# Two orders in a fused attention and gated-FFN kernel: the last v, q and k products of a chunk with their PSUM banks, and the step of an exchanged gate piece

## The chip, the cores and the metric

The kernel runs on one core of one Trainium2 chip. The metric is the device time of one execution in microseconds (us). Times are lower-is-better, and the time before is the median of three runs.

## The reference

One input `x` of 1 x 2048 x 576 in bf16. It is layer-normed, goes through a sliding-window attention of 32 heads of 18 with a window of 256, and through a gated FFN with 4608 hidden columns; the two results are multiplied.

```python
xn = _layernorm(x)
q, k, v = split(xn @ wqkv)                       # 32 heads of 18
p = softmax(mask(q @ k.T * 18 ** -0.5))          # causal, window 256
s = (p @ v) @ wo
g = silu((sigmoid(xn @ w_gate) * (xn @ w_up)) @ w_down)
return x + s * g
```

## The kernel before

**Chunks.** The 2048 tokens are worked in four chunks (c = 0 to 3) of 512 tokens, each of four blocks of 128. A chunk goes through these stages on TensorE (PE): the q, k and v products (line 521), the first FFN product with gate and up (f1, line 898) with the attention's scores (line 688) and the product of probabilities and v (line 745) put between its steps, then the second FFN product (f2, line 1045) with the output projection `wo` (line 815) inside it. The stages of neighbouring chunks overlap: the q, k, v products of chunk c+1 stand between the two halves of f2 of chunk c, that is, behind f2 of blocks 0 and 1 and ahead of f2 of blocks 2 and 3. So there are three such transitions, from chunk 0 to 1, 1 to 2 and 2 to 3.

**One order for all engines.** `schedule` (line 1145) is a list planner. Every operation has an engine, a cost, a priority (a smaller number goes first, at 40 ns a step) and dependencies; each engine takes next the operation that can start first by these costs, and this order is then fixed in the program (`emit`, line 1288). At run time an engine waits on semaphores in that order and does not skip.

**Banks.** PSUM has eight banks of 512 f32 a partition. A `Psum` object lists candidate banks, and the planner takes the candidate that is free first by its costs (`place`, line 1180); of two that are free at the same time it takes the first listed. A bank is free when its last reader is done.

**The transition.** `build_qkv` (line 543) issues twelve products of 1.1 us each, one after the other (`QKV_CHAIN`), in the order of `QKV_NEXT`; q2 waits in order for the second half of `wo` (`QKV_WO`), so six products (to k1) stand ahead of that half and six behind it. Each product takes two banks: (4,5), (6,7), (0,1) or (2,3), unless `QKV_BANKS` gives it a list of its own. What empties the banks differs:

- q is copied by VectorE (DVE) in one piece of 128x576, k by ScalarE (ACT) in one such piece (line 579). Both go into a ring `pk` of three slots, and SyncE (SP) then issues a DMA that transposes the slot into `qkp` (line 604). A slot is free again when its transposing DMA has landed, so the copy of a q or k waits for the DMA of three products of q and k before.
- v is copied in four pieces of 64x288, two by ACT and two by DVE (line 625), into `vau`; no DMA is involved.
- `kd` (line 672) are DVE operations that need the transposed k of two blocks. Those of the first head group on k0 and k1 stand in DVE's order shortly behind the copies of v2, with priority 0 where a copy has 1.

**f2 of blocks 2 and 3** (`build_f2_pair`, line 1029) takes the banks `F2B = ((0, 1), (2, 3))`, both pairs at its first matmul. It runs 17.6 us, and f1 of the next chunk follows, in banks 4 to 7. After the two transposes of q3 and k3, SP issues the loads of the first three weight groups of that f1, twelve DMAs.

**f1** (`build_ffn`, line 858) works in steps: a step is one matmul on rows 0 to 63 of the array (list `low`, the gate tiles) and one on rows 64 to 127 (list `high`, the up tiles), nine steps for a tile of 128 hidden columns. Since 576 is nine pieces of 64, gate and up do not split evenly, and two pieces of one gate tile, number `XS[c]` (13 in chunk 0, 1 in the others), are exchanged into `high`, with weights from `sat`:

```python
n = NC * (xs - 1) + XP[0]
high[n:n] = [(0, xs, 0, 0), (0, xs, 1, 1)]
```

From that step on the gate tile holds a bank of 4 to 7. The steps are issued in runs of two or three, which begin where a tile changes in either list (`cuts`); a run waits at its start for all its weights, for new banks and for a fence: the gate tile's own first run in `low` waits until the exchanged matmuls in `high` are complete. The four loads of a weight group are for rows 0 to 63 positions 0 to 4, rows 64 to 127 positions 0 to 3, then 5 to 8 and 4 to 8. A bank of f1 is emptied by a tanh on ACT (line 912) for gate, and by a multiplication on DVE (line 916) for up.

The scores are released by steps of f1: in chunks 1 to 3 the first after f2 is over, the second behind the first run that begins at step 7 or later, then every 7 steps. They take the banks (0,1) and (2,3).

Of the kernel before, what the change touches and what calls it, by code (L numbers as in the profile page):

```python
# [59 lines left out]
AVOID_NS = 20000.0  # L60
RBN = 4
XS = (13, 1, 1, 1)
XP = (4, 0)
RUN = 3
WX_PRIO = -1
WX_FT = 7
WD_AT = (14, 18, 22, 28, 29, 30, 31, 32, 33)
QKV_FIRST = "q0 q1 v0 v1 q2 v2 k0 v3 k1 q3 k2 k3"
QKV_NEXT = "q0 k0 q1 v0 v1 k1 q2 k2 v2 q3 k3 v3"
QKV_GATE = 2  # L70
QKV_PRIO = -2
QKV_CHAIN = 1
QKV_WO = {"v1": (0,), "q2": (1,)}
WO_QKV = {"k0": (1,)}
QKV_BANKS = {"q3": ((0, 1), (2, 3)), "k3": ((4, 5), (6, 7)), "v3": ((4, 5), (6, 7))}
QKV_F2 = (1, 8)
LAST = 448
W_GATE = 2
# [138 lines left out]
class Builder:  # L217
# [325 lines left out]
    def build_qkv(self, c):  # L543
        self.op_q, self.op_k, self.op_qkt, self.op_qe = [], [], [], []
        old = [o for l in self.op_sc[c - 1] for o in l] + self.op_tail if c > 0 else []
        order = QKV_FIRST if c == 0 else QKV_NEXT
        prev = None
        for w in order.split():
            i, j = int(w[1]), "qkv".index(w[0])
            o = (self.build_v if j == 2 else self.build_qk)(c, i, j, old)  # L550
            if c > 0:
# [5 lines left out]
                for ps in o.alloc:  # L557
                    ps.cands = QKV_BANKS.get(w, ps.cands)
            prev = o
# [298 lines left out]
    def build_ffn(self, c):  # L858
# [7 lines left out]
        for ft in range(NFT):  # L866
            low += [(0, ft, i, None) for i in (gp if ft == xs else range(NC))]
            high += [(1, ft, i, None) for i in (up if ft == xe else range(NC))]
        n = NC * (xs - 1) + XP[0]
        high[n:n] = [(0, xs, 0, 0), (0, xs, 1, 1)]  # L870
        n = len(low) - NC + XP[1]
        low[n:n] = [(1, xe, 0, 0), (1, xe, 1, 1)]
# [534 lines left out]
```

## Time and profile before

| what | us |
|---|---|
| median of three runs (559.4, 560.35, 560.78) | 560.35 |
| the profiled execution | 559.34 |
| its span, first to last instruction | 557.6 |
| around the span | 1.74 |
| PE busy | 551.9 (99% of the span) |
| DVE busy, ACT busy | 312.2, 279.5 |
| q, k, v products, DVE copy of one q | 0.752 (median) |
| DVE copy of one piece of v, ACT copy of one piece of v | 0.458, 0.407 (medians) |
| one `kd` on DVE | 0.281 (median) |

The profiler records one execution. A row of the timeline has its start, its length, the engine, the line of the kernel, the operation with the tiles it writes and reads, the shapes, and in brackets the idle time of that engine before it with what ended it. PEld is the loading of weights into PE, which runs beside its matmuls; "issue" there means that PE's own queue held it. Two matmuls of a step begin within some ns of each other, and the next step begins about 0.216 later when nothing holds it (45.59 and 45.80 in chunk 0).

### The profile page before, as it was taken

How to read it: one execution, taken by the hardware profiler on the slowest of the kernel's cores; microseconds unless marked ns; L12 is line 12 of the kernel's file. 1: busy time of each engine (PE TensorE's matmuls, PEld its weight loads, DVE VectorE, ACT ScalarE, POOL GpSimd, SP SyncE). 2: the span in 40 equal slices, each digit the busy share in tenths (PEclk: the TensorE clock that was granted, in tenths of full speed). 3: DMA queues.
4: the chain of work that ended last, by engine and by line, in shares of the span. 5: the costliest groups of instructions: out<-in, count | busy, mean ns of one | idle time of the engine just before them, and what ended most of it. 6: DMA issues, size and time to landing. Idle time of an engine off the chain costs nothing.

```text
span 557.6 us, 18763 instructions
## 1 busy us (share of the span) xinstructions
PE 551.9 (99%) x8146; PEld 309.8 (56%) x8146; DVE 312.2 (56%) x906; ACT 279.5 (50%) x395; POOL 29.3 (5%) x58
## 2 busy tenths in 40 slices
PE   8999999999999999999999999999999999999997
PEld 5755555567555455556755554545665555554554
DVE  6436998415067988633407798852330785975011
ACT  8436886124076767602308778740330875883021
POOL 3000110100000100010000011001000000000100
PEclk9999999999999999999999999999999999999999
DMA  8999878938945676234993666423399356660010
GB/s 201 221 203 210 209 183 224 232 62 154 209 104 128 148 152 137 53 52 66 176 206 87 151 149 150 105 51 73 60 178 190 90 127 144 133 132 25 20 44 22
DMA packets 125929, 73.35 MB, mean 132 GB/s; under 512 B 54680, under 2 KB 125336, under 8 KB 125848
## 3 DMA queue, kind: packets, MB, share of 16 engines
q1 hardware_dynamic: 125848, 72.16, 61.1%
q8 instruction: 64, 1.05, 0.8%
q14 instruction: 17, 0.14, 0.1%
HBM read 55.48 MB, written 2.36 MB: 104 GB/s over the span
## 4 chain that ended last, share of the span: by engine, by line
PE 98%; DVE 1%; DMA 0%; issue 0%; ACT 0%
PE ps L898 50%; PE ps L1045 22%; PE ps L521 9%; PE ps L688 6%; PE ps L745 4%; PE ps L815 3%; PE ps L1076 2%; PE ps L1100 2%; DMA xr<-in_A_x_dram 0%; DVE bnst L460 0%; DVE bnst L458 0%; DVE xnr L469 0%; PE ps L495 0%; DVE mv L462 0%; ACT expr L1133 0%
## 5 line engine op out<-in xcount | busy, mean ns | idle before, releaser
L898 PE MATMUL ps<-xn,wgs 64*128 64x512 bf16 x2522 | 299.3, 376 | 0.0
L898 PEld LDWEIGHTS ps<-xn,wgs 64*128 64x128 bf16 x2522 | 121.5, 94 | 114.1 <-issue 1.4
L703 ACT ACTIVATE expr<-ps 128x1024 bf16<-128x1024 f32 (+1 forms) x152 | 150.7, 1019 | 23.9 <-PE ps L688 23.8
L916 DVE SCALAR_TENSOR_TENSOR hT<-tring,ps 128x512 bf16<-128x512 bf16 x144 | 98.2, 682 | 54.8 <-PE ps L898 35.1
L912 ACT ACTIVATE tring<-ps 128x512 bf16<-128x512 f32 x144 | 86.5, 600 | 82.3 <-PE ps L898 62.5
L1045 PE MATMUL ps<-wd_sb,hT 64*128 64x512 bf16 (+1 forms) x2016 | 125.5, 283 | 0.1
L1045 PEld LDWEIGHTS ps<-wd_sb,hT 64*128 64x128 bf16 x2016 | 65.8, 94 | 58.8 <-issue 0.4
L717 DVE TENSOR_TENSOR expr<-expr,m 128x256 bf16<-128x256 bf16 (+1 forms) x272 | 61.3, 267 | 6.4 <-ACT expr L703 5.9
L688 PE MATMUL ps<-qkp,kd 64*128 64x320 bf16 (+4 forms) x720 | 56.7, 252 | 0.0
L521 PE MATMUL ps<-wqkv_sb,xn 64*128 64x288 bf16 x864 | 54.4, 283 | 0.0
L688 PEld LDWEIGHTS ps<-qkp,kd 64*128 64x128 bf16 x720 | 34.2, 94 | 33.3 <-issue 0.8
L672 DVE TENSOR_SCALAR kd<-qkp,hm 128x256 bf16<-128x256 bf16 x176 | 40.5, 290 | 15.7 <-DMA qkp<-pk 13.4
L1133 ACT ACTIVATE expr<-ps 128x576 bf16<-128x576 f32 (+2 forms) x17 | 9.8, 620 | 76.9 <-PE ps L1045 61.6
L521 PEld LDWEIGHTS ps<-wqkv_sb,xn 64*128 64x128 bf16 x864 | 42.8, 94 | 9.4
L1135 DVE SCALAR_TENSOR_TENSOR expr<-expr,ps 128x576 bf16<-128x576 bf16 x12 | 8.5, 751 | 66.6 <-ACT expr L1133 66.6
L840 ACT ACTIVATE sat<-ps 128x576 bf16<-128x576 f32 x16 | 9.5, 648 | 65.1 <-PE ps L815 65.1
L1137 DVE TENSOR_TENSOR expr<-expr,sat 128x576 bf16<-128x576 bf16 (+2 forms) x17 | 7.2, 436 | 43.5 <-ACT expr L1133 34.4
L761 DVE STREAM_TRANSPOSE pk<-ps 128x512 f32<-128x512 f32 x32 | 21.4, 696 | 17.2 <-PE ps L745 17.2
L727 POOL COPY qkp<-qkp 128x256 bf16<-128x256 bf16 x24 | 10.2, 427 | 263.7 <-DVE kd L672 263.7
L778 DVE STREAM_TRANSPOSE op__63<-pk 128x512 bf16<-128x512 bf16 x32 | 22.3, 701 | 0.1
L745 PEld LDWEIGHTS ps<-expr,vau 64*32 64x32 bf16 x1440 | 18.1, 92 | 7.4 <-issue 5.5
L745 PE MATMUL ps<-expr,vau 64*32 64x320 bf16 (+4 forms) x1440 | 20.8, 254 | 0.0
(55 smaller groups left out, 222.7 us busy)
## 6 DMA issues: line engine op xcount, KB each, us to landing
wgs<-in_B_w_gate_dram SPq DMA_DIRECT2D x47, 240.0 KB, 3.8
wgs<-in_B_w_up_dram SPq DMA_DIRECT2D x47, 240.0 KB, 4.8
wgs<-in_B_w_up_dram SPq DMA_DIRECT2D x47, 192.0 KB, 4.3
wgs<-in_B_w_gate_dram SPq DMA_DIRECT2D x47, 192.0 KB, 4.7
wd_sb<-in_B_w_down_dram SPq DMA_DIRECT2D x9, 576.0 KB, 6.4
xf<-in_A_x_dram SPq DMA_DIRECT2D x18, 144.0 KB, 2.6
out_dram<-xf SPq DMA_DIRECT2D x15, 144.0 KB, 2.1
xr<-in_A_x_dram SPq DMA_DIRECT2D x14, 144.0 KB, 4.3
```

The source lines that it names most:

```text
L521: r = e.matmul(self.bank(ps, HV, hf), self.xn[r0:r0 + 64, k, i * P:(i + 1) * P], self.wqkv_sb[r0:r0 + 64, j, k, :], start=(k == 0), stop=( ...
L672: return e.tensor_scalar(dst, src, self.hm[:, half:half + 1], None, ALU.mult)
L688: i = e.matmul(self.bank(ps, 512, r)[:, pos * 64:(pos + n) * 64], w, self.qkp[r0:r0 + 64, hg, q0 * 64:(q0 + n) * 64], start=True, stop=Tru ...
L703: return e.activation(self.expr[:, es, :, 0:ncol], src, ACTF.Exp, scale=SM_SCALE)
L717: return e.tensor_tensor(ap, ap, m, ALU.mult)
L745: r = e.matmul(self.bank(ps2[s_])[32 * cg:32 * cg + 32, q0 * 64:(q0 + n) * 64], vf[:, v0:v0 + 32], self.expr[p0:p0 + 64, es, cg % 2, pos * ...
L761: tr = self.rd("DVE", dve_ns(CH), lambda e, tf=tf, s_=s_: e.transpose(tf, self.bank(ps2[s_])), f"t1:{c}:{t}", deps=[o, self.op_mul[c][t - ...
L778: t2 = self.op("DVE", dve_ns(CH), lambda e, on=on: e.transpose(self.op_[:, hg % NOT, :], on.rearrange("p g d -> p (g d)")), f"t2:{c}:{hg}" ...
L898: return e.matmul(self.bank((pg, pu)[gu][ft]), w, self.xn[r0:r0 + 64, i, :], start=first, stop=last, tile_position=(r0, 0))
L912: return e.activation(self.tring[:, st_, :], self.bank(ps), ACTF.Tanh, scale=0.5)
L916: return e.scalar_tensor_tensor(self.hT[:, ft, :], self.tring[:, st_, :], 1.0, self.bank(ps), ALU.add, ALU.mult)
L1045: r = e.matmul(self.ps[:, b + n0:b + n1], self.hT[r0:r0 + 64, ft, i * P:(i + 1) * P], self.wd_sb[r0:r0 + 64, q, ft % WDG, n0:n1], start=(s ...
```

## The change

Three constants change. In the three later chunks v3 is computed ahead of q3 and k3. The bank lists of the last products are exchanged: v2 and v3 may now use only (0,1) and (2,3), those of f2 of blocks 2 and 3; q3 and k3 only (4,5) and (6,7), those of f1. And the two exchanged pieces of gate stand one step later in `high`, behind five instead of four pieces of the up tile, in all four chunks.

```diff
-XP = (4, 0)
+XP = (5, 0)
-QKV_NEXT = "q0 k0 q1 v0 v1 k1 q2 k2 v2 q3 k3 v3"
+QKV_NEXT = "q0 k0 q1 v0 v1 k1 q2 k2 v2 v3 q3 k3"
-QKV_BANKS = {"q3": ((0, 1), (2, 3)), "k3": ((4, 5), (6, 7)), "v3": ((4, 5), (6, 7))}
+QKV_BANKS = {"v2": ((0, 1), (2, 3)), "v3": ((0, 1), (2, 3)), "q3": ((4, 5), (6, 7)), "k3": ((4, 5), (6, 7))}
```

## The prediction

> **What bounds the kernel.** I read the page's busy times first, then the chain and PE's waits, then the timeline where the change cuts in.
>
> ```profile
> span 557.6 us, 18763 instructions
> PE 551.9 (99%) x8146; PEld 309.8 (56%) x8146; DVE 312.2 (56%) x906; ACT 279.5 (50%) x395; POOL 29.3 (5%) x58
> ...
> PEclk9999999999999999999999999999999999999999
> ...
> PE 98%; DVE 1%; DMA 0%; issue 0%; ACT 0%
> ```
>
> ```profile
> PE ps L396 <- DVE hm L381: 1.5, 1, 1.5
> PE ps L495 <- DVE xnr L469: 0.4, 1, 0.4
> PE ps L495 <- DVE mv L462: 0.3, 1, 0.3
> ```
>
> PE is the bound from end to end, at full clock, and the only waits that the profile lists for it (second fence, from the list of waits) are in the first 8 us. But a matmul's end is modelled, so a short wait hides inside "busy". I therefore compared the starts of neighbouring matmuls with their normal pace (0.216 a step of f1, 0.122 a pair of q, k, v). Outside the first 8 us and the v products of the attention, which lose the same time in every group, only two places lose over 0.1 us. Both lie where the change cuts in. The first is in f1 of chunk 0, at gate tile 13:
>
> ```profile
> 44.84 0.60 ACT L912 ACTIVATE tring<-ps 128x512 bf16<-128x512 f32 x1 [1.34 <-PE ps L898]
> ...
> 45.02 0.09 PEld L898 LDWEIGHTS ps<-xn,wgs 64*128 64x128 bf16 x1
> 45.55 0.09 PEld L898 LDWEIGHTS ps<-xn,wgs 64*128 64x128 bf16 x1 [0.44 <-issue]
> ...
> 45.59 0.39 PE L898 MATMUL ps<-xn,sat 64*128 64x512 bf16 x1
> ```
>
> The `sat` matmul is the exchanged piece. Its run needs the bank that the tanh of gate 11 empties at 45.44. PE's queue is held until then, the weights load at 45.55, and the step starts at 45.58; the step before started at 45.22, so 0.36 - 0.216 = **0.15 us** are lost. The second is f2 of blocks 2 and 3 at the transition from chunk 1 to 2:
>
> ```profile
> 273.74 0.48 DVE L672 TENSOR_SCALAR kd<-qkp,hm 128x256 bf16<-128x256 bf16 x2 [1.00 <-DMA qkp<-pk]
> ...
> 274.25 0.76 DVE L579 CAST pk<-ps 128x576 bf16<-128x576 f32 x1
> ...
> 274.68 0.65 ACT L579 ACTIVATE pk<-ps 128x576 bf16<-128x576 f32 x1 [2.04 <-DMA qkp<-pk]
> ...
> 275.13 0.36 PEld L1045 LDWEIGHTS ps<-wd_sb,hT 64*128 64x128 bf16 x6 [0.38 <-issue]
> 275.16 0.61 PE L1045 MATMUL ps<-wd_sb,hT 64*128 64x512 bf16 x4
> ```
>
> f2 waits for the copy of q3 (DVE, 274.25, over at 275.01), which sits in (2,3). That copy is late: v2 was copied from 271.79, q3's product was ready one product (1.10) later, near 272.9, but two `kd` stand ahead of it and wait until 273.72 for the transposed k1. The last q, k, v pair started at 274.77, so f2 was due at 274.90 and lost **0.26 us**. The other two transitions have the same order and lose nothing:
>
> ```profile
> 135.76 0.48 DVE L672 TENSOR_SCALAR kd<-qkp,hm 128x256 bf16<-128x256 bf16 x2 [0.30 <-DMA qkp<-pk]
> 136.27 0.76 DVE L579 CAST pk<-ps 128x576 bf16<-128x576 f32 x1
> ...
> 137.61 0.59 PE L1045 MATMUL ps<-wd_sb,hT 64*128 64x512 bf16 x4
> ...
> 410.33 0.48 DVE L672 TENSOR_SCALAR kd<-qkp,hm 128x256 bf16<-128x256 bf16 x2
> 410.85 0.76 DVE L579 CAST pk<-ps 128x576 bf16<-128x576 f32 x1
> ...
> 412.46 0.59 PE L1045 MATMUL ps<-wd_sb,hT 64*128 64x512 bf16 x4
> ```
>
> So 0.41 us is all that the two places can give back.
>
> **The change, part by part.**
>
> *Exchanged piece one step later.* The matmuls are the same; one up step goes ahead of two exchanged ones. In chunk 0 the piece is then due one step later, at 45.43 + 0.216 = 45.65, and the bank lets it start at 45.58: the whole 0.15 goes (bounds: 0 and -0.15). Two waits move. The run of three steps now waits for the group's fourth weight load four steps earlier; in chunk 0 those loads land by 37.6, 7 us ahead, and in chunk 1 by 147.8 against an f1 that starts at 155.25. And the fence is nearer: three steps, 0.648, from the last exchanged matmul to the gate tile's own first, instead of four. It needs the matmul's 0.376 and then some 0.135 from a semaphore to a matmul (45.44 to 45.58 above), 0.51 in all, so 0.14 is left: nothing. In chunks 1 to 3 a score unit of 0.22 stands between as well, and the bank at step 4 had been free for long: nothing either way. The score's gate at step 7 opens one run earlier, but its banks are free only when DVE has read blocks 2 and 3 of f2 (two multiplications from 156.14 to 157.56), and the second unit starts at 157.84 already: nothing.
>
> *v3 ahead of q3 and k3.* Product 10 of 12 is now v3. v2's shorter list changes nothing: it takes (0,1), the first to come free behind `wo`. v3 takes what q3 took, (2,3); q3 follows `wo` into (4,5), and k3 gets (6,7), which q2 or k2 has left. f2 now waits for v2 and v3 instead of v2 and q3. v3 is ready at the same time as q3 was, near 272.9, with the same priority, so in DVE's order I expect it **behind the same two `kd`**. Its DVE part is two copies of 0.458 with 0.03 between, 0.95, for one copy of 0.76: +0.19. ACT's two pieces (0.407 each) stand ahead of k3's copy and are done by 273.8. Per transition: 1 to 2 starts f2 at 275.16 + 0.19 = 275.35 and loses 0.45; 0 to 1 has the second copy done at 136.27 + 0.95 = 137.22, and the weights of f2 load from 137.49: 0.27 in hand; 2 to 3 has it at 410.85 + 0.95 = 411.80 against 412.34. So **+0.19** in all. Bounds: -0.26 (v3's copies ahead of the `kd`) and three times +0.19 = +0.57.
>
> *q3 and k3 later.* Their products end one product (1.1) later, q3's copy stands behind v3's two, and its transposing DMA, issued at 275.04, leaves about 1.0 later; k3's at 276.32 and the twelve weight loads behind it on SP, from 277.79, move by up to 1.0. k3's copy waits less for its slot in `pk`. Cover: the first weight group has landed at 286.1 of 292.8 when f1 starts, k3's transpose at 279.6, and DVE has only `kd` between that and 292. This would cost something only from 6.7 us of delay on: 0.
>
> Sum: -0.15 + 0.19 = **+0.04 us** on a profiled execution of 559.34 (span 557.6 and 1.74 around it). That execution is 1.0 below the median and just under the lowest of the runs shown, so I put the step on the median: 560.35 + 0.04 = **560.4**.
>
> One rule of the Trainium skill bears on the step I trust least. Its page "PSUM — Partial Sum Buffer" (section "Engine vs sequencer instructions") says that VectorE's queue is strictly first in, first out. It speaks against this change: a free bank partner does not help when the copy is queued behind a waiting `kd`, and the sum is +0.04; if a ready copy could pass, it would be -0.41. The trace agrees: q3's copy, ready near 272.9, starts 0.03 behind the second `kd`.
>
> **The rivals.**
>
> 1. *Both losses go*: -0.15 - 0.26 = -0.41, 559.9. For it: v3's copies need no transposed k, so an order with them ahead of `kd` is legal. Against: `kd` has the better priority and stood ahead of an equal copy. 0.16.
> 2. *v3's longer copy is late in more transitions.* From a landing of k1 to the end of v3's copies are 0.02 + 0.48 + 0.03 + 0.95 = 1.48 us; the spare is 0.27 and 0.54 at the other two. k1's transposes took 4.4, 4.6 and 3.3 us from issue to landing. With 4.6 plus some tenths at all three: -0.15 + 0.57 = +0.42, 560.8. 0.22.
> 3. *Slower for certain: the first scores move ahead of the first tanh.* Had the earlier gate put the second score unit into step 9, ACT would run its exponential (0.97 each in "157.89 1.93 ... x2") ahead of the tanh that frees a gate bank (157.40 to 158.00, needed by step 16 near 159.1), and DVE's products shift with it: up to 1.0 a chunk, three chunks, +3 at most, 563.4; it decides from DVE's reading of blocks 2 and 3 ending before 157.2, where the trace has 157.56. Any other re-planning of f1 that costs PE would look alike. 0.08.
> 4. *It doesn't do what it says:* the exchanged piece waits for a weight load or the fence instead of the bank, 0.15 stays: +0.19, 560.5; inside 2's width, counted there.
>
> **How the numbers follow.** Main case 0.50, rivals 0.16, 0.22 and 0.08, and 0.04 for a gain that I cannot place. About 0.3%, 1.7 us, is what a measurement of this kernel can tell from no change; main case and rivals 1, 2 and 4 are all within it: 0.88. Slower 0.08, faster 0.04. The range takes in -0.41 and +0.42 around 560.4 and a scatter of the median like that of the runs shown (0.95 down, 0.43 up), cut where two in ten are left out: 559.4 to 561.3.
>
> **What would show it.** In the changed profile: the `sat` matmul of chunk 0 starts one pace behind its neighbour and PEld's 0.44 is gone; in DVE's order behind v2's copies come two `kd`, two copies of v3, then q3's; at the transition 1 to 2 PEld still shows "issue" ahead of L1045, longer than 0.38 if k1 lands as late as here; k3's transposes land about 1 us later with nobody waiting. It would be wrong if v3's copies stand ahead of `kd`, or if PE shows a new wait in f1.

## The result and the profile after

The changed kernel takes 562.16 us in the median of 22 runs (559.67 to 566.78), the kernel before in as many runs beside it 560.34 (559.22 to 561.5). The ratio is 1.0035, with a 95% interval of 1.0023 to 1.0047: about 2 us **slower**, just past the 0.3% that count as a difference here, and with a wider scatter than before. Two of the 22 runs took over 566, at a granted clock of 0.996 and 0.997 where the others have 0.999 or more; what they lost beyond the rest is not known, since only one execution has a profile. The profiled execution took 561.7, its span is 560.0 against 557.6.

The page of the changed kernel looks like that of before until one reaches the chain, where PE has gone from 98% to 94% and DMA and SP's queue have come in:

```profile
span 560.0 us, 18756 instructions
...
PE 553.0 (99%) x8144; PEld 312.6 (56%) x8146; DVE 311.7 (56%) x906; ACT 280.1 (50%) x395; POOL 30.7 (5%) x58
...
PEclk9999999999999999999999999999999999999999
...
PE 94%; DMA 2%; SPq 1%; DVE 1%; ACT 1%; issue 0%; DVEq 0%
```

PE's list of waits has two lines over 0.2 us that the list of before lacks (columns: who waited for whom, total, times, longest):

```profile
PE ps L688 <- DVE expr L1135: 0.9, 1, 0.9
PE ps L1045 <- DVE vau L625: 0.6, 1, 0.6
```

The second is the forecast one, f2's start at the transition 1 to 2, with v3's copies behind the two `kd`:

```profile
274.55 0.48 DVE L672 TENSOR_SCALAR kd<-qkp,hm 128x256 bf16<-128x256 bf16 x2 [1.31 <-DMA qkp<-pk]
275.07 0.94 DVE L625 CAST vau<-ps 64x288 bf16<-64x288 f32 x2
...
276.16 0.61 PE L1045 MATMUL ps<-wd_sb,hT 64*128 64x512 bf16 x4 [0.60 <-DVE vau L625]
```

The first is new: a **score** (L688) waits for DVE's reading of the banks that f2 of blocks 2 and 3 leaves (L1135). With the starts of neighbouring matmuls, as in the prediction, the 2.3 us between the two spans (557.61 and 559.95) come apart like this:

| place | before, us lost | after, us lost | change |
|---|---|---|---|
| gate tile 13, chunk 0 | 0.15 | 0 | -0.15 |
| start of f2 of blocks 2 and 3, transition 1 to 2 | 0.26 | 0.76 | +0.50 |
| first score, chunk 1 (start, us into f1) | 1.94 | 2.18 | +0.24 |
| first score, chunk 2 | 1.94 | 3.05 | +1.11 |
| first score, chunk 3 | 1.94 | 2.15 | +0.21 |
| start of the program up to f1 of chunk 0 | 21.26 | 21.69 | +0.43 |

The last line is scatter: the ten profiles of this study have f1 of chunk 0 start between 21.26 and 21.69. So 1.56 of the loss lies at the first scores. The timeline of chunk 2's first steps shows what came ahead of them:

```profile
293.80 1.46 PE L898 MATMUL ps<-xn,wgs 64*128 64x512 bf16 x11
294.01 1.19 ACT L1133 ACTIVATE expr<-ps 128x576 bf16<-128x576 f32 x2 [17.69 <-PE ps L1045]
...
295.55 0.48 DVE L672 TENSOR_SCALAR kd<-qkp,hm 128x256 bf16<-128x256 bf16 x2 [18.75 <-DMA qkp<-pk]
295.95 1.41 DVE L1135 SCALAR_TENSOR_TENSOR expr<-expr,ps 128x576 bf16<-128x576 bf16 x2
...
296.85 0.40 PE L688 MATMUL ps<-qkp,kd 64*128 64x320 bf16 x4 [0.93 <-DVE expr L1135]
```

DVE stood still for 18.75 us, for two `kd` that need the transposed k3. L1135 had its input from ACT at 294.66 but is queued behind them, and the score waits for L1135. In the kernel before these `kd` ran at 279.73 and L1135 at 293.70. And k3's transpose is late because of SP. SP's queue before (first fence) and after (second):

```profile
275.04 2.70 SPq L256 DMA_TRANSPOSE qkp<-pk  x2
277.79 0.62 SPq L257 DMA_DIRECT2D wgs<-in_B_w_gate_dram  x1
```

```profile
276.83 1.23 SPq L256 DMA_TRANSPOSE qkp<-pk  x1
278.11 0.62 SPq L257 DMA_DIRECT2D wgs<-in_B_w_gate_dram  x1
...
285.72 0.62 SPq L257 DMA_DIRECT2D wgs<-in_B_w_up_dram  x1
286.38 3.81 SPq L256 DMA_TRANSPOSE qkp<-pk  x1
```

Before, q3's and k3's transposes go out one after the other (x2), then the twelve weight loads. After, k3's goes out **behind all twelve**, at 286.38, though ACT had copied k3 by 276.32. It is also slower there: it lands at 295.46, 9.07 us after its issue, where before it took 3.32.

### The profile page after: what moved, and what is told of

Its sections match the earlier page's. It is cut to its first block, busy times and chain, and to the rows that moved or that the text cites. A ratio compares the mean times of both kernels' runs of the same rounds, so it can differ in the third digit from the quotient of the medians.

```text
span 560.0 us, 18756 instructions
## 1 busy us (share of the span) xinstructions
PE 553.0 (99%) x8144; PEld 312.6 (56%) x8146; DVE 311.7 (56%) x906; ACT 280.1 (50%) x395; POOL 30.7 (5%) x58
## 3 DMA queue, kind: packets, MB, share of 16 engines
q8 instruction: 64, 1.05, 0.9%
## 4 chain that ended last, share of the span: by engine, by line
PE 94%; DMA 2%; SPq 1%; DVE 1%; ACT 1%; issue 0%; DVEq 0%
PE ps L898 50%; PE ps L1045 19%; PE ps L521 8%; PE ps L688 6%; PE ps L745 4%; PE ps L815 3%; DMA qkp<-pk 2%; PE ps L1100 2%; PE ps L1076 2%; SPq L257 1%; PE ps L396 1%; ACT xn L507 0%; DVE kd L672 0%; DVE vau L625 0%; ACT sat L840 0%
## 5 line engine op out<-in xcount | busy, mean ns | idle before, releaser
L898 PEld LDWEIGHTS ps<-xn,wgs 64*128 64x128 bf16 x2522 | 123.8, 94 | 111.9 <-issue 1.1
L1045 PE MATMUL ps<-wd_sb,hT 64*128 64x512 bf16 (+1 forms) x2016 | 125.5, 283 | 0.6 <-DVE vau L625 0.6
L1045 PEld LDWEIGHTS ps<-wd_sb,hT 64*128 64x128 bf16 x2016 | 65.7, 94 | 59.4 <-issue 0.9
L688 PE MATMUL ps<-qkp,kd 64*128 64x320 bf16 (+4 forms) x720 | 56.8, 252 | 1.0 <-DVE expr L1135 0.9
L688 PEld LDWEIGHTS ps<-qkp,kd 64*128 64x128 bf16 x720 | 34.4, 94 | 34.6 <-issue 3.2
L1137 DVE TENSOR_TENSOR expr<-expr,sat 128x576 bf16<-128x576 bf16 (+2 forms) x17 | 7.2, 437 | 43.6 <-ACT expr L1133 34.4
L727 POOL COPY qkp<-qkp 128x256 bf16<-128x256 bf16 x24 | 11.4, 477 | 264.1 <-DVE kd L672 264.1
L1135 DVE SCALAR_TENSOR_TENSOR expr<-expr,ps 128x576 bf16<-128x576 bf16 x12 | 8.5, 750 | 26.7 <-ACT expr L1133 26.7
```

The source lines that it names most:

```text
L688: i = e.matmul(self.bank(ps, 512, r)[:, pos * 64:(pos + n) * 64], w, self.qkp[r0:r0 + 64, hg, q0 * 64:(q0 + n) * 64], start=True, stop=Tru ...
L898: return e.matmul(self.bank((pg, pu)[gu][ft]), w, self.xn[r0:r0 + 64, i, :], start=first, stop=last, tile_position=(r0, 0))
L1045: r = e.matmul(self.ps[:, b + n0:b + n1], self.hT[r0:r0 + 64, ft, i * P:(i + 1) * P], self.wd_sb[r0:r0 + 64, q, ft % WDG, n0:n1], start=(s ...
```

## The experiments

Theory A: the loss is k3's transposing DMA behind the weight loads, passed on through DVE's queue. Theory B: it is f2's longer wait for v3's two copies. Theory C: it is the exchanged piece's later step, to which I also put down a shift of scores within f1. The ratio is to the kernel before, run on the same chip in the same job.

### The order and banks alone

```diff
 (of the changed kernel)
-XP = (5, 0)
+XP = (4, 0)
```

> The new order and banks of the last products, with the exchanged piece where it was. Theory A (SP's order: k3's transposing DMA now stands behind the twelve weight loads, and its kd hold DVE ahead of the reading of f2's last banks): the whole loss stays, +1.5 to +2.3 us, and the first score of chunks 1 to 3 waits 0.2 to 1.5 us in the profile. Theory B (f2 waits longer for v3's two copies): also about +0.5 us in all, but the first scores don't wait. Theory C (the exchanged piece's later step): the loss is gone, within 0.3 us of before.

Measured: 562.31 (561.08 to 563.39), ratio 1.0035 (1.0024 to 1.0047). The whole loss is there without the piece, and the first scores of chunks 1 to 3 come 0.15, 1.05 and 0.26 us late. f2 loses 1.28 at the transition 1 to 2 in this trace. C falls.

### The exchanged piece alone

```diff
 (of the kernel before)
-XP = (4, 0)
+XP = (5, 0)
```

> The exchanged piece one step later, with the old order and banks. Theories A and B: -0.15 us, from the wait at gate tile 13 of chunk 0, which is gone; within 0.3 us of before by the timing. Theory C: +1.5 to +2.3 us.

Measured: 559.62, ratio 0.9992 (0.9983 to 1.0001). In its trace the step at gate tile 13 loses nothing, and f2 loses the same 0.26 at the transition 1 to 2 as in the kernel before. The step of the piece is worth its 0.15 in the trace; the timing alone can't tell it from nothing.

### k3's transpose ahead of the weight loads again

```diff
 (of the changed kernel, in build_qk)
-deps=ev + old, prio=0, issue=XT_ISSUE_NS, transpose=True)
+deps=ev + old, prio=-3 if (i, j) == (3, 1) else 0, issue=XT_ISSUE_NS, transpose=True)
```

> The changed kernel with one priority altered, so that SP issues k3's transposing DMA ahead of the twelve weight loads again. Theory A: the first scores do not wait, and what is left is the forecast, +0.04 us (0 to +0.6, as k1's transpose lands). Theory B: f2's wait of 0.3 to 0.8 us stays and with it the whole +1.8 us. Theory C: +1.8 us stays.

Measured: 560.42, ratio 0.9998 (0.9989 to 1.0007). The loss is gone with one priority. The trace has both transposes together on SP, `kd` 13 us ahead of L1135, and the first scores 1.94 us into f1 in all three chunks:

```profile
276.43 2.62 SPq L256 DMA_TRANSPOSE qkp<-pk  x2
```

```profile
281.11 0.48 DVE L673 TENSOR_SCALAR kd<-qkp,hm 128x256 bf16<-128x256 bf16 x2 [4.71 <-DMA qkp<-pk]
294.29 1.42 DVE L1136 SCALAR_TENSOR_TENSOR expr<-expr,ps 128x576 bf16<-128x576 bf16 x2 [12.70 <-ACT expr L1134]
```

f2 still loses 0.72 at the transition 1 to 2, so B's wait is real, but it isn't the loss of 2 us.

### The kernel before, with k3's transpose behind the loads

```diff
 (of the kernel before, in build_ffn, behind the loads of a weight group)
+if c > 0 and fg == RW - 1:
+    self.op_qkt[-1].behind = ws[-1:]
```

> The kernel before with one thing altered: SP issues k3's transposing DMA of chunks 1 to 3 behind the twelve weight loads. Theory A: +1.5 to +2.3 us as in the changed kernel, with the first score of chunks 1 to 3 waiting. Theories B and C: no change, within 0.3 us.

Measured: 561.3, ratio 1.0024 (1.0015 to 1.0033): +1.3 us, a little under the lowest that A had said, from nothing but the place of one DMA. The first scores of chunks 1 and 2 wait, those of chunk 3 don't (there the transpose landed at 433.18, 0.13 us into f1, and L1135 started at 433.93, 0.88 into f1, as it always does):

```profile
287.23 3.76 SPq L256 DMA_TRANSPOSE qkp<-pk  x1
```

```profile
PE ps L688 <- DVE expr L1137: 1.1, 2, 0.8
...
PE ps L521 <- ACT pk L579: 0.6, 1, 0.6
PE ps L1047 <- DVE pk L579: 0.5, 1, 0.5
```

(L1137 and L1047 are L1135 and L1045 of the kernel before, two lines further down.) A holds in both directions: putting the DMA back takes the loss away, and moving it in the old kernel makes most of it.

### The transpose late, but its kd behind the bank readings

```diff
 (of the changed kernel, in build_kd; op_fq1 collects the operations of line 1135)
+if c > 0 and hg == 0 and g == 2:
+    self.ops_kd[g][-1].odeps += self.op_fq1[-2:]
```

> The changed kernel; k3's transposing DMA stays behind the twelve weight loads, but the kd of k2 and k3 of the first head group are put behind DVE's two readings of f2's last banks (line 1135). If the loss goes through DVE's queue, the first score of chunks 1 to 3 no longer waits (it comes 1.94 us into f1, as before) though the transpose lands as late; the third score unit, the first that needs these kd, may wait instead where the transpose lands more than 4 us into f1. About +0.3 us against before (the wait at f2's start is left), at most +0.8. If the first score waits for the transpose itself, or the late DMA costs something else, the +1.8 us stays.

Measured: 560.13, ratio 0.9993 (0.9985 to 1.0001). The transpose is as late as ever (issued at 287.26, landed at 296.13), and it costs nothing:

```profile
295.33 1.42 DVE L1138 SCALAR_TENSOR_TENSOR expr<-expr,ps 128x576 bf16<-128x576 bf16 x2 [17.89 <-ACT expr L1136]
296.67 0.45 DVE L1141 TENSOR_TENSOR expr<-expr,sat 128x576 bf16<-128x576 bf16 x1
297.04 0.28 DVE L673 TENSOR_SCALAR kd<-qkp,hm 128x256 bf16<-128x256 bf16 x1
```

L1138 (L1135 of before) now starts 0.89 us after f1's start at 294.44, as it did before (293.70 against 292.80), and the first score comes 1.94 us in. The time is a little under the +0.3 that was expected, although f2 loses 1.05 at the transition 1 to 2 in this trace. So the late data hurt no reader of their own; they hurt the two operations queued behind the first one that waited for them.

### The transpose behind four loads

```diff
 (of the kernel before, in build_ffn, with the priority of k3's transpose at -3 too)
+if c > 0 and fg == 0:
+    self.op_qkt[-1].behind = ws[-1:]
```

> The kernel before; SP issues k3's transposing DMA of chunks 1 to 3 behind the first four of the twelve weight loads. If what counts is the landing against the end of f2, it lands 5 us or more before f2 is over and the time is that of before (within 0.3 us). If any place behind weight loads costs, +0.5 to +1.4 us.

Measured: 559.87, ratio 0.9993 (0.9984 to 1.0001). Issued at 280.84 and landed at 286.36, its `kd` run 9 us before L1135 (here L1138):

```profile
286.46 0.48 DVE L673 TENSOR_SCALAR kd<-qkp,hm 128x256 bf16<-128x256 bf16 x2 [8.62 <-DMA qkp<-pk]
295.55 1.42 DVE L1138 SCALAR_TENSOR_TENSOR expr<-expr,ps 128x576 bf16<-128x576 bf16 x2 [8.60 <-ACT expr L1136]
```

At the other two transitions it also lands 8 us ahead of f1 (148.00 against 156.45, 423.81 against 431.95). So being behind loads costs nothing by itself; what counts is that its `kd` are done before L1135 is due.

### v3's copies ahead of the kd on k1

```diff
 (of the changed kernel with k3's transpose first, in build_kd)
+if c > 0 and hg == 0 and g == 1:
+    self.ops_kd[g][-1].odeps += self.op_v[c * QPC + QPC - 1][2:]
```

> The changed kernel with k3's transposing DMA ahead of the weight loads, and the two kd on k0 and k1 behind v3's copies in DVE's order. If f2's late start at the transition 1 to 2 is DVE's queue (0.73 us in the kernel with k3's DMA first alone), it is gone: -0.4 us against before, and f2 loses nothing at all three transitions. If f2 waits for something else, 0.3 us or more stays.

Measured: **559.1 (558.92 to 559.29), ratio 0.9979 (0.9971 to 0.9988)**, against 560.29 (559.05 to 561.75) beside it: 1.2 us faster than before, the best version found.

```profile
273.10 0.94 DVE L626 CAST vau<-ps 64x288 bf16<-64x288 f32 x2 [0.15 <-PE ps L521]
274.57 0.48 DVE L673 TENSOR_SCALAR kd<-qkp,hm 128x256 bf16<-128x256 bf16 x2 [0.53 <-DMA qkp<-pk]
```

```profile
271.92 3.04 PEld L521 LDWEIGHTS ps<-wqkv_sb,xn 64*128 64x128 bf16 x50
274.98 1.11 PEld L1048 LDWEIGHTS ps<-wd_sb,hT 64*128 64x128 bf16 x14
```

The second copy of v3 is over at 274.04, half a us before `kd` may start, and PEld goes from the products to f2 (L1048) without a gap. f2 loses nothing at any transition. The gain is larger than the 0.4 of the forecast, which went by one profile. The eleven runs lie within 0.37 us of each other, those of before within 2.7; that fits waits for k1's landing which in other executions of the kernel before were longer than in the profiled one. The executions without a profile can't be looked into, but two other profiles with the old order (the transpose late in the kernel before, and behind four loads) show 0.69 and 0.89 lost at f2's start where the kernel before shows 0.26.

### The old order, with q3's copy ahead of the kd

```diff
 (of the kernel before with the piece one step later, in build_kd; op_q3e is q3's copy)
+if c > 0 and hg == 0 and g == 1:
+    self.ops_kd[g][-1].odeps += self.op_q3e
```

> The old order and banks, the exchanged piece one step later, and the two kd on k0 and k1 behind q3's copy in DVE's order. If that queue is the cause, f2 loses nothing at the transition 1 to 2 without any change of the order of products: -0.4 us against before. Otherwise the 0.26 us stays, and it is -0.15 us.

Measured: 559.54 (558.97 to 560.58), ratio 0.9987 (0.9978 to 0.9997): 0.75 us faster than before, 0.15 of it by the trace from the piece, f2 without a loss in its trace. The wait at f2's start needs no new order of products to go; q3's copy has only to stand ahead of the waiting `kd`. q3's copy has a wait of its own, for its slot in `pk`, which k1 holds until the same landing: in this trace it starts at 273.70, 0.02 after k1 has landed. v3's copies have none. That would be an advantage of the new order once the two queues are right, but it is argued, not shown: the intervals of these last two versions overlap.

## Why the prediction was wrong

Forecast 560.4, range 559.4 to 561.3, slower by over 0.3% with a chance of 0.08; measured 562.16.

- **The step that failed** is "q3 and k3 later": "k3's at 276.32 and the twelve weight loads behind it on SP ... move by up to 1.0". I moved the DMA in time and took its place in SP's order as given. By the costs in `schedule`, q3's transpose moves as well, and this decides it. In the plan of the changed kernel (planner's times of the transition 1 to 2, not measured ones) q3's transpose holds SP until 275.41. k3's is ready at 275.12, but the loads, which f2's first matmuls release, are ready at 275.38, 0.03 before SP is free. Then both stand ready, the loads have priority -2 and the transpose 0, and all twelve go first. In the plan of the kernel before, SP is free early enough to start k3's transpose at 274.93, 0.48 before the loads are released. Both priorities are in the code that issues these DMAs, and the experiment that alters the one of k3's transpose turns the order back. What I called covered up to "6.7 us of delay" was issued 10.1 us later and landed 15.8 us later (295.46 against 279.63).
- In the same step I noted that "DVE has only `kd` between that and 292" and stopped there. The question was what stands *behind* those `kd`: L1135, at 293.7, which frees the banks of the first scores. The experiment with `kd` behind L1135 shows that the loss goes this way alone.
- **f2's start**: the mechanism was right, the size not. Forecast were 0.45 lost, 0.19 more than before; measured are 0.76, 0.50 more. v3's two copies did stand behind the two `kd` and did cost 0.19 more than q3's one: in the four profiles with the old order that keep the `kd` ahead, f2 starts 1.44 us behind k1's landing, in the four with the new order 1.63. The other 0.31 is k1's transpose, which landed 0.87 us before f2 was due (274.53 and 275.40) instead of 1.18 (273.72 and 274.90). It is this margin that varies: f2 loses 0.26, 0.26, 0.69 and 0.89 in the four old ones, 0.72, 0.76, 1.05 and 1.28 in the four new ones, so the 0.26 that I set out from was the low end. The other two transitions lost nothing, as forecast. One reading was wrong: q3's copy was not ready near 272.9, since its slot in `pk` is k1's and came free only at the same landing (the last experiment shows this wait), so the two `kd` cost it 0.5 us and not 1.3. The rule that was weighed there from the page "PSUM — Partial Sum Buffer" of the Trainium skill (section "Engine vs sequencer instructions"), VectorE's queue as first in, first out, held for v3: ACT copied its two pieces from 273.40, DVE its own only from 275.07, behind the `kd`. The same rule, applied to L1135 behind `kd`, gives the loss that I missed.
- **The exchanged piece**: right. The 0.15 is gone, and neither the nearer fence nor the earlier weight load shows. PEld still has 0.23 of "issue" there, not none, but it delays no matmul. In chunk 2 three of the later score units stand two steps further on, which I had not forecast; that comes from the new order (with the piece alone no score moves), and with k3's transpose ahead it costs nothing.
- **The rivals**: the third named the first scores as the place, but by an earlier start; it was a later one. The first, both losses gone, is what the best version does, for which the DVE order had to be changed by hand.
- **The range** was built from bounds on the waits that I had found. A plan that is made anew can turn round two operations on any queue, and a bound for that, k3's transpose behind the loads, could have been worked out from the rows: twelve issues of 0.66 are 8 us, more than the 6.7 that I had given as the cover. It would have flagged the step without giving its size: 6.7 is the cover of the weights, and k3's transpose itself had 13.6 us in the kernel before, from its landing at 279.63 to 0.49 (the two `kd`) ahead of L1135 at 293.70. The 10.1 us of later issue alone fit into that; it was the landing behind the loads, 9.07 us after the issue in place of 3.32, that went beyond it.

## What to carry to other kernels

When a product is moved in a kernel whose queues are ordered by a planner, go through every queue that its followers enter, the DMA queue above all, and ask with the planner's own priorities who is ready beside them then; a shift of one us can become the length of everything that is let past. A late transfer costs what is queued behind its first waiter, not only what reads it: look for the next operation on that engine which frees a bank. And a wait that differs from run to run, as one for a DMA's landing does, can be larger in the median than in the one execution that a profile shows.

## What the runs showed of the hardware

- The transpose of k3 into `qkp` landed 3.2 to 3.3 us after its issue ahead of the loads (kernel before), 4.9 to 5.5 behind four loads of 192 or 240 KB, and 7.7 to 9.1 behind twelve. SP's own issue of it took 1.3 to 1.4 us ahead of the loads, 1.3 to 1.5 behind four, and 3.2 to 4.7 behind twelve. The Trainium skill's page "DMA: Bandwidth & Descriptors" (section "Queues, rings and completion order") says that a DMA engine takes the descriptors of a ring in order, by which a transfer behind bulk loads would wait for them. The landings agree: in chunk 2 of the changed kernel the last of the twelve loads landed at 293.04, the transpose at 295.46.
- In four of the ten profiles (the order alone, k3's transpose behind twelve and behind four loads in the kernel before, and `kd` behind L1135) PE loses 0.75 to 0.92 us at 135 us, at the tenth product of the first transition: its bank is k2's, whose copy by ACT waits for its `pk` slot. That slot is held by q1's transpose, which in these four landed 4.9 to 5.1 us after its issue and in the other six 3.2 to 3.5. It comes with the old and the new order. Why the landing has these two values stays open; it was not tried.
